# Attention and the first six expert jobs under one table of dates; routing steps on GpSimd; sums of squares in SBUF

## The chip, the cores and the metric

The kernel runs on one NeuronCore of a Trainium2 chip. The metric is the device time of one execution in microseconds (us). Engines are named as in the profile: PE is TensorE (PEld its weight loads), DVE is VectorE, ACT is ScalarE, POOL is GpSimd, SP is SyncE, which here issues most of the DMAs. Each engine works through its own instructions in program order; an instruction that waits holds up all that stand behind it.

## The reference

Attention with RMS-normalised queries and keys, whose output is the token matrix of a mixture of experts with 4 groups of 4 experts, one of the 16 chosen for each token (top group, then top expert in it).

```python
q, k: (8, 12, 448, 64); v the same              # batch, heads, sequence, head size
q_n, k_n = rmsnorm(q, g_q), rmsnorm(k, g_k)     # x / sqrt(mean(x*x) + 1e-6) * g
attn = softmax(q_n @ k_n^T / sqrt(64)) @ v
x = attn.transpose(0, 2, 1, 3).reshape(3584, 768)
g_idx = argmax(x @ w_group); e_idx = argmax(x @ w_expert[g_idx])    # both with a softmax weight
out[token] = g_w * e_w * (relu(x[token] @ w1[g, e]) @ w2[g, e])     # w1: 768 x 1024, w2: 1024 x 768
```

All inputs and the output are fp32. The kernel splits most operands into a high and a low 16-bit half and multiplies three times.

## The kernel before

**Attention** is cut into 16 units of six heads (half a batch entry). For a unit SP loads q, k and v; ACT squares q and k (`sq`), DVE adds the squares up (`red`, line 247), ACT and DVE make 1/rms of the sums (`rs1`, lines 255 and 256; `rs2`, lines 260 to 262) and DVE multiplies it in (`norm_k`, `norm_q`, line 265). The sums and 1/rms lie in 42 spare columns of one of the two PSUM banks `po` into which PE also adds up the attention's output (line 597). ACT rounds k to its high half, POOL (in places DVE) takes the low one (`kn`, line 280), and DMAs transpose. PE makes scores once for the row maximum (`pmx`, which DVE reduces, `mx`, line 480) and once for the softmax (`pss`), of which ACT takes the exponential (`p`, line 546) and POOL or DVE the low half (`pl`, line 552); PE multiplies them with v (`po`, line 597). DVE or ACT scale the result into `xm`, ACT and POOL (or DVE) split it (`xhl`, lines 660 and 664), and SP stores it to a DRAM matrix `x16`.

**Routing** follows in five groups of 128-token chunks: three of seven chunks, then three and four. For each chunk `x16` is read transposed and multiplied with the gate weights (`prl`); then one chain of 20 steps (`choices`, lines 934 to 989), of which all but two are DVE's, finds the expert, the slot in its list and the token's weight, and POOL writes them by indirect DMA to a table in DRAM (`tab`). After the third group `order.early` (DVE) picks the two fullest experts, on which work may start before the last tokens are routed. After the last group `order.final` sorts all sixteen (`order`, line 1101).

**Experts** run as 18 jobs: 0 and 1 are the early rows of the first two experts (256 and 224 rows), 2 and 3 their later rows (96 and 64), 4 to 17 one expert each. A job reads its rows' numbers (POOL, line 1287 or 1292), gathers the tokens by indirect DMA (`xg`, line 1310), transposes them by DMA into `mx` (line 1417), and PE multiplies them with w1 (line 1321) and w2 (line 1340). An expert's weights come as eight pieces of 768 KB (`stage`, line 1268) that ACT rounds to high halves (line 1274) and DVE to low halves (line 1275). Two sets of 16-bit weights take turns.

**The order of the work** is written out. Every piece of attention and routing is a task of `Flow`, which names the engine, the tasks that it follows and the buffers that it takes; the table `PLAN` gives each task a date, and a star picks its second engine. The dates set only the order in which instructions are recorded, and so their order on each engine. The expert jobs are not tasks: `Moe.plan` gives them dates of its own (`MO`, and 2.5/6 ns for each column of a matmul) beside those of the attention. The memory of the experts' first weights is opened when the last task that uses the early buffers is recorded, that of the rest after the last `po` matmul.

Of the kernel before, what the change touches and what calls it, by code (L numbers as in the profile page):

```python
# [21 lines left out]
P = 128  # L22
# [42 lines left out]
class Flow:  # L65

    def __init__(self, room):
        self.room, self.tasks = room, []  # L70
# [33 lines left out]
class Attention:  # L104
# [8 lines left out]
                psd=3, psx=2, pso=2, p=7, xm=1, hl=1, rx=2)  # L113
# [111 lines left out]
    def plan_prep(self, flow, u, B, D):  # L225
# [20 lines left out]
        def red(nm, o, a, e):  # L246
            nc.vector.tensor_reduce(rms()[:, o + a:o + e], d["sq" + nm][:, a:e], axis=AX.X, op=ALU.add)  # L247
# [3 lines left out]
        def rs1(a=0, e=N):  # L251
            if a == 0:
                d["y"] = self.wk.tile([P, 2 * N], F32, tag="y", name=f"y{u}")
            y, x = both_(d["y"], a, e), both_(rms(), a, e)
            nc.scalar.activation(y, x, AF.Ln, scale=1.0 / 1024, bias=self.eps)
            nc.scalar.activation(y, y, AF.Exp, scale=-0.5)

        def rs2(a=0, e=N):
            y, x = both_(d["y"], a, e), both_(rms(), a, e)
            nc.vector.scalar_tensor_tensor(x, x, 64e-6, y, op0=ALU.add, op1=ALU.mult)  # L260
            nc.vector.scalar_tensor_tensor(x, x, -0.5 / 1024, y, op0=ALU.mult, op1=ALU.mult)
            nc.vector.scalar_tensor_tensor(x, x, 1.5, y, op0=ALU.add, op1=ALU.mult)
# [144 lines left out]
    def plan_first(self, add, D, B, N, F, both, d):  # L407
# [12 lines left out]
        for i in range(NPR):  # L420
# [5 lines left out]
            for nm, o in (("k", N), ("q", 0)):  # L426
                x = task("sq" + nm, "ACT", pair(F["sq"], nm, a, e), [ld[nm]], takes=[B["sq" + nm]], uses=[B["n" + nm]])
# [140 lines left out]
    def plan_av(self, flow, u, B, D):  # L568
# [56 lines left out]
        for i in range(NPR):  # L625
# [10 lines left out]
            D["x"].append(flow.add(evac_on, lambda g, i=i: evac(g, i), [x], uses=[bo] + ([] if i else []),  # L636
# [43 lines left out]
    def plan(self, flow, router, order):  # L680
# [3 lines left out]
        add("ACT", lambda: nc.scalar.preload_act_table_set("natural_log_exp_and_others"))  # L684
# [9 lines left out]
        for u in range(U):  # L694
# [16 lines left out]
            Ds.append(D)  # L711
        for g, (a, e) in enumerate(router.groups):
            last = 2 * ((e * P - 1) // self.S) + 1
            if g == 3:
                self.early = add("DVE", lambda: order.early(router.bank, router.groups[2][1]), done, takes=[Buffer("psd")])
                done = [self.early, *done]
# [9 lines left out]
class Router:  # L726
# [26 lines left out]
    def init(self):  # L753
# [9 lines left out]
        self.tok = cp.tile([P, NC], I32, tag="tok", name="tok")  # L763
        nc.gpsimd.iota(self.tok, pattern=[[P, NC]], base=0, channel_multiplier=1)
# [40 lines left out]
    def plan_last(self, flow, a, e, Ds, done, room):  # L805
# [11 lines left out]
        def logits(d, wk):  # L817
# [57 lines left out]
            def sum_():  # L875
# [5 lines left out]
            t0 = [add("SP", lambda i=i, l=l: tr(i, l), [at(U - 4), at(U - 2)],  # L881
                      takes=rx if i + l == 0 else (), uses=() if i + l == 0 else rx) for i in range(2) for l in range(2)]
# [3 lines left out]
            t1 = [add("SP", lambda l=l: tr_tail(l), [at(U - 3)], takes=() if l else ry, uses=ry if l else ())  # L886
                  for l in range(2)]
# [14 lines left out]
    def plan(self, flow, a, e, stores, done, room, logits=None):  # L902

        nc = self.nc
        n = e - a
# [22 lines left out]
        def choices():  # L928
# [3 lines left out]
            v, bc = nc.vector, lambda t: t.unsqueeze(2).to_broadcast([P, S, E])  # L932
# [3 lines left out]
            v.tensor_tensor(D, L, bc(m), op=ALU.subtract)  # L936
# [13 lines left out]
            for j in range(n):  # L950
                v.tensor_tensor(oh[:, j], one[:, j, 1:, :], one[:, j, 0, :].unsqueeze(2).to_broadcast([P, G, E]), op=ALU.mult)
# [12 lines left out]
            v.tensor_tensor(q, o, oh, op=ALU.mult)  # L964
# [683 lines left out]
```

## Time and profile before

| | |
|---|---|
| time, median of three runs | 1061.61 us (1059.2 to 1064.75) |
| the profiled execution | 1068.18 us, of which the span of its instructions is 1066.4 us |
| busy in the span: PE, DVE, ACT, POOL | 922.6, 769.7, 597.4, 516.3 us |
| mean granted TensorE clock | 0.96 of full speed |
| last `po` matmul ends, first expert matmul starts | 535.1 us |
| job 6 starts on PE | 707.5 us |

A row of a group of instructions reads: line, engine, operation, out<-in by the program's names, sizes, count | busy time, mean ns of one | idle time of the engine ahead of them and what ended it. Busy times of neighbours overlap a little, since an instruction starts while the one ahead drains.

### The profile page before, as it was taken

Reading aid. Unit: us, or ns where it says so; the run is one execution under the profiler, and the core shown is the slowest. Engines: PE = TensorE matmul, PEld = TensorE weight load, DVE = VectorE, ACT = ScalarE, POOL = GpSimd, SP = SyncE. Lnnn points to the kernel's source line nnn. Section 1 sums busy time; section 2 is a strip of 40 time slices with the busy share of each in tenths; the row PEclk is TensorE's granted clock in tenths of the full one; section 3 lists DMA queues with packets and bytes.
Section 4 is the critical chain, followed back from the end, with each engine's and each line's share of the span. In section 5 each row is a group of like instructions: output and inputs, shape, how many; then the busy total and the mean of one; then the engine's idle time right before and its main releaser. Section 6 shows DMA issues by size and latency. Waiting matters only on the chain.

```text
span 1066.4 us, 27993 instructions
## 1 busy us (share of the span) xinstructions
PE 922.6 (87%) x11425; PEld 649.0 (61%) x11425; DVE 769.7 (72%) x1087; ACT 597.4 (56%) x962; POOL 516.3 (48%) x428
## 2 busy tenths in 40 slices
PE   1678899888896888977788989989999999999995
PEld 0335566545563555545575766766877777778883
DVE  5999899999899987977946256758666475766520
ACT  5757788667675775444734245544554465545520
POOL 5448888758874786554513441432612131433411
PEclk9989999989998999997889989999999999999998
DMA  6698999996997679834978399998999999999900
GB/s 168 161 196 195 185 212 198 202 196 159 200 192 156 146 170 197 131 90 77 252 178 251 107 317 295 323 241 288 296 316 245 311 259 295 308 278 299 283 29 26
DMA packets 298419, 224.74 MB, mean 211 GB/s; under 512 B 172015, under 2 KB 271333, under 8 KB 298288
## 3 DMA queue, kind: packets, MB, share of 16 engines
q1 hardware_dynamic: 288336, 199.24, 74.9%
q0 software_dynamic: 8608, 22.99, 7.0%
q8 instruction: 91, 1.49, 0.6%
q10 hardware_dynamic: 1344, 0.69, 0.3%
q14 instruction: 40, 0.33, 0.1%
HBM read 145.69 MB, written 23.41 MB: 159 GB/s over the span
## 4 chain that ended last, share of the span: by engine, by line
PE 51%; DVE 20%; DMA 12%; issue 7%; ACT 5%; SPq 3%; POOL 1%; another core or an unknown queue 1%; ACTq 0%; DVEq 0%; POOLq 0%
PE ps L1321 19%; PE ps L1340 15%; PE po L597 5%; PE pss L536 5%; DVE mx L480 4%; DMA mx<-xg 4%; PE pmx L475 3%; DVE po L247 2%; DVE w1l L1275 2%; DVE ql L308 1%; DMA xg<-x,tb 1%; DVE vl L346 1%; PE pss L531 1%; DVE qp L265 1%; DMA vn<-v 1%
## 5 line engine op out<-in xcount | busy, mean ns | idle before, releaser
L552 POOL TENSOR_TENSOR pl<-p 128x896 f16<-128x896 f32 (+1 forms) x143 | 238.1, 1681 | 132.0 <-ACT p L546 119.3
L1321 PE MATMUL ps<-mx,w1h 128*128 128x256 f16 (+6 forms) x1728 | 250.0, 261 | 15.0 <-DMA mx<-xg 10.6
L1321 PE MATMUL ps<-mx,w1l 128*128 128x256 f16 (+6 forms) x864 | 215.9, 261 | 0.0
L546 ACT ACTIVATE p<-pss 128x896 f32<-128x896 f32 (+1 forms) x177 | 153.3, 881 | 96.5 <-PE pss L536 70.4
L480 DVE TENSOR_REDUCE mx<-pmx 128x2 f32<-128x896 f32 (+1 forms) x177 | 177.7, 1033 | 18.4 <-PE pmx L475 16.3
L597 PEld LDWEIGHTS <-p 128*128 128x128 bf16 (+1 forms) x3072 | 150.7, 104 | 61.6 <-issue 40.2
L1321 PEld LDWEIGHTS <-w1h 128*128 128x128 f16 x1728 | 159.1, 100 | 34.0 <-issue 9.8
L597 PE MATMUL po<-vh,p 128*128 128x65 f16 (+1 forms) x1536 | 159.1, 200 | 13.6 <-DVE qp L265 7.4
L1340 PE MATMUL ps<-w2l,hh 128*128 128x384 f16 (+2 forms) x768 | 164.9, 303 | 3.0 <-issue 3.0
L1340 PE MATMUL ps<-w2h,hh 128*128 128x384 f16 (+2 forms) x768 | 164.4, 305 | 1.3 <-issue 1.3
L597 PE MATMUL po<-vh,pl 128*128 128x65 f16 (+1 forms) x1536 | 157.6, 197 | 8.5 <-DVE pl L552 6.5
L1340 PE MATMUL ps<-w2h,hl 128*128 128x384 f16 (+2 forms) x768 | 163.8, 303 | 0.0
L1275 DVE SCALAR_TENSOR_TENSOR w2l<-stage,w2h 128x1536 f16<-128x1536 f32 x64 | 112.3, 1754 | 64.3 <-ACT w2h L1274 63.0
L597 PE MATMUL po<-vl,p 128*128 128x64 f16 (+1 forms) x1536 | 157.8, 196 | 0.2 <-issue 0.2
L1324 ACT ACTIVATE hh<-ps 128x256 f16<-128x256 f32 (+6 forms) x144 | 49.5, 349 | 172.9 <-PE ps L1321 158.9
L1340 PEld LDWEIGHTS <-hh 128*128 128x128 f16 (+2 forms) x1536 | 101.7, 100 | 64.5 <-issue 10.6
L1275 DVE SCALAR_TENSOR_TENSOR w1l<-stage,w1h 128x1536 f16<-128x1536 f32 x64 | 112.9, 1786 | 32.4 <-ACT w1h L1274 31.7
L597 PEld LDWEIGHTS <-pl 128*128 128x128 f16 (+1 forms) x1536 | 130.1, 103 | 9.8 <-DVE pl L552 6.9
L1351 POOL DMA_INDIRECT out<-y,tb x23 | 32.2, 1401 | 201.0 <-DVE y L1346 102.5
L536 PE MATMUL pss<-qa,kt 128*128 128x448 f16 x288 | 106.5, 370 | 22.8 <-DVE mx L480 17.8
L1310 POOL DMA_INDIRECT xg<-x,tb x41 | 69.4, 1692 | 101.0 <-DMA mx<-xg 48.3
L536 PE MATMUL pss<-qb,kb 128*128 128x448 f16 x288 | 106.4, 369 | 5.8 <-DMA qb<-mxt 5.8
(195 smaller groups left out, 1525.4 us busy)
## 6 DMA issues: line engine op xcount, KB each, us to landing
stage<-w SPq DMA_DIRECT2D x128, 768.0 KB
vn<-v SPq DMA_DIRECT2D x16, 576.0 KB
x<-xhl SPq DMA_DIRECT2D x16, 576.0 KB
nk<-k SPq DMA_DIRECT2D x30, 288.0 KB
nq<-q SPq DMA_DIRECT2D x30, 288.0 KB
qa<-qh SPq DMA_DIRECT2D x30, 176.0 KB
kb<-kt SPq DMA_DIRECT2D x15, 336.0 KB
qa<-qh SPq DMA_DIRECT2D x30, 160.0 KB
```

What stands on the lines that cost most here:

```text
L475: nc.tensor.matmul(s[:, n - a, 0:448], qa[:, n * P:(n + 1) * P], kt[:, x:z], start=True, stop=True)
L480: nc.vector.tensor_reduce(d["mx"][:, a:e], d.pop(("mm", a))[:, 0:e - a, 0:448], axis=AX.X, op=ALU.max)
L536: nc.tensor.matmul(s[:, n - a, 0:448], w[:, n * P:(n + 1) * P], mv[:, x:z], start=first, stop=not first)
L546: nc.scalar.activation(p[:, 0:e - a], s, AF.Exp, scale=1.0 / 64)
L552: ENG[eng].tensor_tensor(l[:, 0:n], p[:, 0:n], h[:, 0:n], op=ALU.subtract)
L597: nc.tensor.matmul(o[op, c, 0:nn], w, mv, start=st, stop=sp, skip_group_check=True)
L1275: self.nc.vector.scalar_tensor_tensor(lo, t, 64.0, hi, op0=ALU.mult, op1=ALU.subtract)
L1310: self.nc.gpsimd.indirect_dma_start(g[0:m], None, self.x16[0:n], bass.IndirectOffsetOnAxis(ap=tb[0:m, i, 0:1], axis=0), bounds_check=n - 1 ...
L1321: nc.tensor.matmul(s[:, 0:c], wb[w][:, i, fs], x[:, l + i, o:o + c], start=i + j == 0, stop=i == DC - 1 and j == 2)
L1324: nc.scalar.activation(hh, s[:, 0:c], AF.Relu)
L1340: nc.tensor.matmul(s[q * m:q * m + m, 0:n], self.h[h][:, f, a:a + m], wb[w][:, f, o:o + n], start=f + j == 0, stop=f == self.FC - 1 and j ...
L1351: i = self.nc.gpsimd.indirect_dma_start(out, bass.IndirectOffsetOnAxis(ap=idx, axis=0), d.pop(("y", i))[:, 0:self.D // r], None, bounds_ch ...
```

## The change

What it does, part by part:

1. `Moe.plan_early` makes the first six jobs tasks of the same `Flow`, and the table `PLAN` is new for all tasks (2512 instead of 2176). The opening of the experts' memory is a task too. `Moe.plan` still dates jobs 6 to 17 as before. The weight split and the relu are cut into ACT's and DVE's part, so that each has a date of its own.
2. In `choices` six steps of each of the three groups of seven chunks go from DVE to POOL (the difference to the maximum, the product of the choices in one instruction instead of seven, two additions, one product, one cast), the test for zero and the product with the priority become one DVE instruction, and a copy is gone. `order.early` is cut into eight steps over PE, DVE and POOL.
3. The sums of squares go to an SBUF tile `ss`; the exponential in `rs1` writes 1/rms to the `po` bank, where the first guess and the result of `rs2` stay.
4. The first task on ACT loads the table set that holds both the logarithm and the exponential, and the first squares depend on it: the built program has one ACT_TABLE_LOAD instead of eight.
5. By the new table 14 of the 16 units' low halves `xhl` are POOL's (before 9), 142 of 177 `pl` (before 143), and 26 of 30 `kn` (before 27).

```diff
-        add("ACT", lambda: nc.scalar.preload_act_table_set("natural_log_exp_and_others"))
+        self.table = add("ACT", lambda: nc.scalar.preload_act_table_set("natural_log_exp_and_others"))
...
-            nc.vector.tensor_reduce(rms()[:, o + a:o + e], d["sq" + nm][:, a:e], axis=AX.X, op=ALU.add)
+            nc.vector.tensor_reduce(d["ss"][:, o + a:o + e], d["sq" + nm][:, a:e], axis=AX.X, op=ALU.add)
...
-            y, x = both_(d["y"], a, e), both_(rms(), a, e)
+            y, x, z = (both_(t, a, e) for t in (d["y"], d["ss"], rms()))
             nc.scalar.activation(y, x, AF.Ln, scale=1.0 / 1024, bias=self.eps)
-            nc.scalar.activation(y, y, AF.Exp, scale=-0.5)
+            nc.scalar.activation(z, y, AF.Exp, scale=-0.5)
...
-            v, bc = nc.vector, lambda t: t.unsqueeze(2).to_broadcast([P, S, E])
+            v, g, bc = nc.vector, nc.gpsimd if side else nc.vector, lambda t: t.unsqueeze(2).to_broadcast([P, S, E])
...
-            v.tensor_tensor(D, L, bc(m), op=ALU.subtract)
+            g.tensor_tensor(D, L, bc(m), op=ALU.subtract)
...
-            v.tensor_scalar(D, D, 0.0, None, op0=ALU.is_equal)
-            yield
-            v.tensor_tensor(c, D, self.prio.unsqueeze(1).to_broadcast([P, S, E]), op=ALU.mult)
+            v.scalar_tensor_tensor(c, D, 0.0, self.prio.unsqueeze(1).to_broadcast([P, S, E]), op0=ALU.is_equal, op1=ALU.mult)
...
-            for j in range(n):
-                v.tensor_tensor(oh[:, j], one[:, j, 1:, :], one[:, j, 0, :].unsqueeze(2).to_broadcast([P, G, E]), op=ALU.mult)
+            g.tensor_tensor(oh, one[:, :, 1:, :], one[:, :, 0, :].unsqueeze(3).to_broadcast([P, n, G, E]), op=ALU.mult)
...
-            v.tensor_scalar(s, s, 1e-9, None, op0=ALU.add)
+            g.tensor_scalar(s, s, 1e-9, None, op0=ALU.add)
-            v.tensor_tensor(self.run, self.run, r, op=ALU.add)
+            g.tensor_tensor(self.run, self.run, r, op=ALU.add)
-            v.tensor_tensor(t, one[:, :, 0, :], W[:, :, 1:], op=ALU.mult)
+            g.tensor_tensor(t, one[:, :, 0, :], W[:, :, 1:], op=ALU.mult)
-            v.tensor_copy(d["slot"], w)
+            g.tensor_copy(d["slot"], w)
-            v.tensor_copy(row[:, :, 0], self.tok[:, a:e])
...
+    EARLY = ("PE", "DVE", "DVE", "POOL", "DVE", "POOL", "DVE", "POOL")
...
+    def plan_early(self, flow, attn, router, opens):
+        m1 = add("NONE", opens[0], flow.using(early))
+        m2 = add("NONE", opens[1], [m1, *flow.using(late)])
+        m3 = add("NONE", opens[2], [m2, *flow.using(lambda b: b.kind == "pso")])
...
+                x = add("SP", lambda k=k, i=i, st=st: self.w_load(self.expert(k, nc.sync), PC[i], self.stage[st], nc.sync),
+                        [attn.early if k < 2 else attn.final, m1 if k == 0 else m2], takes=[b])
+                x = add("ACT", lambda k=k, i=i, st=st: self.w_split(wb(k), PC[i], self.stage[st], 0), [x, m1 if k == 0 else m2, *free], uses=[b])
+                x = add("DVE", lambda k=k, i=i, st=st: self.w_split(wb(k), PC[i], self.stage[st], 1), [x], uses=[b])
...
+                x = mm[j, f] = add("PE", lambda j=j, f=f, k=k, c=c, s=s: s.update(p=self.mm1(wb(k), self.xb[j % 2], f, c, self.col[j])),
+                                   [m2, sets[k][f // 2], *([*trs, *([mm[j - 1, FC - 1]] if j else [])] if f == 0 else [mm[j, f - 1]])], takes=[b])
...
-2366 0 1211 6349 10381 11581 12046 518 1563 1 2 880 945 927 1014 1083 1151 1229 1301 1400 1464* 1581 1372 1711 1811
+210 553 1020 7396 9043 13116 15028 1620 3045 0 1 424 485 486 550 731 915 1030 1136 1480 1997* 2088 1482 1615 2089 1776
```

Place one, DVE at the routing of the first group of seven chunks (`rl` are its logits, `rm` to `roh` the chain's results). Before:

```order
L934 TENSOR_REDUCE rm_3516<-rl_2476 128x35
L936 TENSOR_TENSOR rd_3517<-rl_2476,rm_3516 128x140
L346 SCALAR_TENSOR_TENSOR vl_3471<-vn_133,vh_130 128x768
L940 TENSOR_SCALAR rd_3517<-rd_3517 128x140
L942 TENSOR_TENSOR rc_3519<-rd_3517,prio 128x140
L944 TENSOR_REDUCE rcm_3520<-rc_3519 128x35
L946 TENSOR_TENSOR rd_3517<-rc_3519,rcm_3520 128x140
L308 SCALAR_TENSOR_TENSOR ql_3546<-pqt_1_3541,ghc,qh_3545 128x384
L308 SCALAR_TENSOR_TENSOR ql_3546<-pqt_0_3507,ghc,qh_3545 128x1024
L951 TENSOR_TENSOR roh_3644<-rd_3517 128x16 x7
```

DVE at the same place in the change (`rm` is 13 instructions ahead of `rc`):

```order
L356 SCALAR_TENSOR_TENSOR vl_3864<-vn_133,vh_130 128x768
L270 SCALAR_TENSOR_TENSOR ss_3719<-ss_3719,po_111 128x42
L271 SCALAR_TENSOR_TENSOR ss_3719<-ss_3719,po_111 128x42
L272 SCALAR_TENSOR_TENSOR po_111<-ss_3719,po_111 128x42
L957 SCALAR_TENSOR_TENSOR rc_3834<-rd_3832,prio 128x140
L275 TENSOR_TENSOR nk_3412<-nk_3412,po_111 128x640
L275 TENSOR_TENSOR nk_3412<-nk_3412,po_111 128x704
L959 TENSOR_REDUCE rcm_3835<-rc_3834 128x35
L612 TENSOR_SCALAR rr_2_4034<-po_112 128x7
L613 RECIPROCAL rr_2_4034<-rr_2_4034 128x7
L490 TENSOR_REDUCE mx_3717<-pmx_12_4031 128x2
L961 TENSOR_TENSOR rd_3832<-rc_3834,rcm_3835 128x140
```

POOL at that place in the change:

```order
L562 TENSOR_TENSOR pl_20_3829<-p_20_3828 128x448
L953 TENSOR_TENSOR rd_3832<-rl_2696,rm_3831 128x140
L562 TENSOR_TENSOR pl_4_3867<-p_4_3866 128x896
L562 TENSOR_TENSOR pl_0_3845<-p_0_3844 128x896
L562 TENSOR_TENSOR pl_2_3990<-p_2_3989 128x896
L562 TENSOR_TENSOR pl_6_4014<-p_6_4013 128x896
L562 TENSOR_TENSOR pl_12_4021<-p_12_4020 128x896
L965 TENSOR_TENSOR roh_4102<-rd_3832 128x112
```

The difference and the product have moved to POOL, each behind one or more `pl`; DVE's remaining steps of the chain now stand apart, with other work between.

Place two, ACT at the end of attention (`p` are the last unit's exponentials, `w1h` the first expert's weights). Before:

```order
L546 ACTIVATE p_8_9532<-pss_8_9518 128x896
L660 ACTIVATE xhl_9548<-xm_9079 128x3x384
L660 ACTIVATE xhl_9548<-xm_9079 128x192
L546 ACTIVATE p_12_9577<-pss_12_9526 128x896
L1274 ACTIVATE w1h_9198<-stage_9203 128x6x256
L546 ACTIVATE p_14_9646<-pss_14_9624 128x896
L1274 ACTIVATE w1h_9198<-stage_9204 128x6x256
L546 ACTIVATE p_16_9674<-pss_16_9649 128x896
L546 ACTIVATE p_18_9698<-pss_18_9680 128x896
L1274 ACTIVATE w1h_9198<-stage_9205 128x6x256
L546 ACTIVATE p_20_9792<-pss_20_9776 128x448
L1274 ACTIVATE w1h_9198<-stage_9206 128x6x256
```

And in the change:

```order
L556 ACTIVATE p_8_9432<-pss_8_9424 128x896
L1314 ACTIVATE w1h_9202<-stage_9209 128x6x256
L943 ACTIVATE rl_9097<-prl_9470 128x20
L556 ACTIVATE p_12_9574<-pss_12_9452 128x896
L955 ACTIVATE rx_9509<-rd_9508 128x60
L670 ACTIVATE xhl_9639<-xm_9034 128x3x384
L670 ACTIVATE xhl_9639<-xm_9034 128x192
L556 ACTIVATE p_14_9642<-pss_14_9618 128x896
L556 ACTIVATE p_16_9666<-pss_16_9645 128x896
L556 ACTIVATE p_18_9676<-pss_18_9671 128x896
L556 ACTIVATE p_20_9718<-pss_20_9715 128x448
L1314 ACTIVATE w1h_9202<-stage_9207 128x6x256
```

Three weight splits stood ahead of the last exponential; now one does, but it stands ahead of five exponentials instead of four. On DVE four low halves `w1l` stood ahead of the last `pl`, now one.

## Rows read from the trace of the kernel before

**Rows 1.** The page: busy time of PE, DVE and POOL (us, share of the span, instructions), and the shares of the chain of work that ended last.

```profile
PE 922.6 (87%) x11425; PEld 649.0 (61%) x11425; DVE 769.7 (72%) x1087; ACT 597.4 (56%) x962; POOL 516.3 (48%) x428
PE 51%; DVE 20%; DMA 12%; issue 7%; ACT 5%; SPq 3%; POOL 1%; another core or an unknown queue 1%; ACTq 0%; DVEq 0%; POOLq 0%
```

**Rows 2.** Busy time of each engine by stretches of the span: from and to, length, PE busy (instructions), PEld, DVE, ACT, POOL, granted clock, DMA share, GB/s.

```profile
0.00:72.00 72.00, 34.84 (x256) 16.83 (x256) 56.09 (x76) 44.61 (x69) 35.84 (x58) 0.93 0.73 173
72.00:200.00 128.00, 115.95 (x1807) 73.98 (x1807) 120.27 (x169) 98.99 (x183) 103.50 (x76) 1.00 0.95 196
200.00:360.00 160.00, 131.96 (x2029) 84.44 (x2027) 149.12 (x221) 108.62 (x206) 109.60 (x71) 0.94 0.87 183
360.00:535.10 175.10, 142.58 (x2340) 93.60 (x2337) 146.04 (x234) 102.60 (x192) 107.13 (x80) 0.92 0.69 152
535.10:707.50 172.40, 154.74 (x1740) 116.22 (x1736) 99.19 (x161) 78.00 (x112) 59.34 (x57) 0.95 0.84 241
707.50:1056.00 348.50, 342.56 (x3264) 263.96 (x3264) 198.64 (x230) 164.55 (x204) 99.87 (x87) 1.00 0.87 257
```

**Rows 3.** The chain of work that ended last, in order of time: start, us, what.

```profile
19.19 1.28 ACT L255
...
26.60 1.28 ACT L255
28.18 1.28 ACT L256
...
506.32 9.65 DMA stage<-w
...
535.14 5.67 PE ps L1321 x36
...
569.47 9.00 issue
578.46 3.79 DMA mx<-xg
582.39 15.64 PE ps L1321 x144
...
707.52 19.73 PE ps L1321 x144
...
1041.22 13.64 PE ps L1340 x173
```

**Rows 4.** DVE's groups of instructions, shapes apart: those of routing that the change moves or merges, the low halves that move between DVE and POOL, and the weight split.

```profile
L1275 DVE SCALAR_TENSOR_TENSOR w1l<-stage,w1h 128x1536 f16<-128x1536 f32 x64 | 112.9, 1786 | 32.4 <-ACT w1h L1274 31.7 <-issue 0.6
L346 DVE SCALAR_TENSOR_TENSOR vl<-vn,vh 128x768 f16<-128x768 f32 x32 | 37.0, 1155 | 0.0
L552 DVE TENSOR_TENSOR pl<-p 128x896 f16<-128x896 f32 x30 | 35.2, 1186 | 5.2 <-ACT p L546 5.1
...
L951 DVE TENSOR_TENSOR roh<-rd 128x16 f16<-128x16 f32 x28 | 12.4, 506 | 0.0
...
L664 DVE TENSOR_TENSOR xhl<-xm,xhl 128x1152 f16<-128x1152 f32 x7 | 9.8, 1396 | 0.0
...
L664 DVE TENSOR_TENSOR xhl<-xm,xhl 128x192 f16<-128x192 f32 x7 | 5.4, 774 | 0.0
...
L940 DVE TENSOR_SCALAR rd<-rd 128x140 f32<-128x140 f32 x3 | 3.6, 1214 | 0.0
...
L280 DVE TENSOR_TENSOR kn<-nk,kn 128x704 f16<-128x704 f32 x2 | 3.2, 1622 | 0.0
...
L982 DVE CAST slot<-rv 128x7 int32<-128x7 f32 x3 | 2.3, 777 | 0.1
L979 DVE TENSOR_TENSOR rt<-rd,rs 128x28 f32<-128x28 f32 x3 | 2.3, 760 | 0.0
...
L1085 DVE COPY ooh<-ogt 1x32 f32<-1x32 f32 x1 | 1.7, 1669 | 0.0
...
L969 DVE TENSOR_SCALAR rs<-rs 128x35 f32<-128x35 f32 x3 | 1.3, 440 | 0.0
...
L987 DVE COPY row<-tok 128x7 int32<-128x7 int32 x3 | 1.1, 373 | 0.0
```

**Rows 5.** DVE in order of time near the end of attention (start, us, instruction): the same two kinds of instruction, short and long.

```profile
516.12 1.09 DVE L552 TENSOR_TENSOR pl<-p 128x896 f16<-128x896 f32 x1
...
521.28 2.57 DVE L552 TENSOR_TENSOR pl<-p 128x896 f16<-128x896 f32 x1
...
524.08 2.93 DVE L1275 SCALAR_TENSOR_TENSOR w1l<-stage,w1h 128x1536 f16<-128x1536 f32 x1
```

**Rows 6.** POOL's groups: the low halves of p and of the output.

```profile
L552 POOL TENSOR_TENSOR pl<-p 128x896 f16<-128x896 f32 x129 | 224.8, 1758 | 119.4 <-ACT p L546 106.8 <-issue 4.3 <-DMA qa<-qh 3.6
...
L664 POOL TENSOR_TENSOR xhl<-xm,xhl 128x1152 f16<-128x1152 f32 x9 | 21.7, 2406 | 2.4 <-ACT xhl L660 2.4
...
L664 POOL TENSOR_TENSOR xhl<-xm,xhl 128x192 f16<-128x192 f32 x9 | 5.0, 556 | 0.0
```

**Rows 7.** ACT in order of time: a table load and the activation behind it.

```profile
9.40 1.28 ACT L255 ACT_TABLE_LOAD   x1 [0.18 <-DVE po L247]
10.70 0.27 ACT L255 ACTIVATE y<-po,eps 128x14 f32<-128x14 f32 x1
```

**Rows 8.** DVE in order of time: the cast with which the order of the experts is known.

```profile
581.34 0.16 DVE L1101 CAST order<-oof 1x16 int32<-1x16 f32 x1
```

More of the change, by code (lines that the diff above doesn't have):

```diff
@@ L65 @@
 class Flow:
+    TURNS = ("nv", "vh", "kt", "kb", "qa", "qb", "pso", *(f"st{i}" for i in range(7)), "gb0", "gb1")
     def __init__(self, room):
-        self.room, self.tasks = room, []
+        self.room, self.tasks, self.turn = room, [], {}
     def add(self, engines, f, deps=(), takes=(), uses=()):
@@ L77, in add, with using @@
             b.users.append(t)
+        for b in takes:
+            if b.kind in self.TURNS:
+                t.deps += [x for x in self.turn.get(b.kind, ()) if x not in t.deps]
+                self.turn[b.kind] = [t]
         self.tasks.append(t)
         return t
+    def using(self, pick):
+        return [t for t in self.tasks if any(pick(b) for b in t.uses)]
     def place(self):
@@ L714, in plan @@
             if g == 3:
-                self.early = add("DVE", lambda: order.early(router.bank, router.groups[2][1]), done, takes=[Buffer("psd")])
-                done = [self.early, *done]
+                steps, bp, x = order.early(router.bank, router.groups[2][1]), Buffer("psd"), None
+                for j, on in enumerate(order.EARLY):
+                    x = add(on, lambda: next(steps, None), [x, *([] if j else done)], takes=[] if j else [bp], uses=[bp] if j == 1 else [])
+                self.early = x
+                done = [x, *done]
             stores = lambda j, a=a: [s for b in sorted({((a + j) * P) // self.S, ((a + j + 1) * P - 1) // self.S})
@@ L1003, in plan @@
             x = add("SP", lambda j=j: tr(j), stores(j), takes=[bx])
[L1004 to L1005 removed]
+            x = add("PE", lambda j=j: mm(j), [x, self.ready, first], takes=[bp] + ([] if j else [rl]), uses=[bx])
+            first = first or x
+            cps.append(add("ACT", lambda j=j: cp(j), [x], uses=[bp, rl]))
         c = choices()
         x, bp = None, Buffer(room)
[L1008 to L1011 removed]
+        for j in range(19):
+            on = "ACT" if j == 2 else "PE" if j == 7 else "POOL" if side and j in (1, 6, 11, 12, 15, 16) else "DVE"
+            x = add(on, lambda: next(c, None), [x, *(done + cps if j == 0 else [])],
+                    takes=[bp] if j == 7 else (), uses=[bp] if j == 8 else [rl] if j < 2 else ())
+        self.puts.append([add("POOL", lambda j=j: put(j), [x]) for j in range(n)])
+        return [x, *self.puts[-1]]
 class Order:
@@ new lines, in early @@
+        ix, key = self.ix[:, 0:NE], self.key
+        sq = [1, NE, NE]
+        gt, rk, t = self.oh, self.tile("ork", [1, NE]), self.tile("pick", [1, NE, NE])
+        t2, n, s = self.tile("pick2", [1, 2, NE]), self.tile("onum", [1, NE]), self.tile("ost2", [1, 2])
+        assert r.routed == chunks
+        p = bank("pcnt")
+        nc.tensor.matmul(p[0:1, 0:NE], r.ones[:, 0:1], r.run, start=True, stop=True)
+        yield
+        v.scalar_tensor_tensor(key, p[0:1, 0:NE], 16.0, self.kb, op0=ALU.mult, op1=ALU.add)
@@ L1434, in plan @@
         for i in range(30):
-            at(T[5] + 3000.0 * i, lambda: next(rest, None))
+            at(T[6] + 3000.0 * i, lambda: next(rest, None))
     def rest(self):
@@ L1613, in body @@
         attn.plan(flow, router, order)
-        flow.place()
-        flow.emit(agenda, STEP)
-        begun = lambda pick: max(t.start for t in flow.tasks if pick(t)) / STEP
-        kinds = lambda ks: lambda t: any(b.kind in ks for b in t.uses)
-        at = agenda.at(0)
         def banks():
```

402 lines of the change are left out of this document (240 added, 162 removed), and 125 rows, old and new, of the table PLAN.

## The prediction

> **What bounds the kernel now.** I read the page first: PE is busy 87% of the span and holds half of the chain that ended last, DVE 72% and a fifth of it [rows 1]. These are means over stages, so I next cut the span where the chain changes hands: at 535.1 us, where the last attention matmul ends and the first expert matmul begins, and at 707.5 us, where job 6 starts [rows 3]. The busy times by stretch [rows 2] show three limits. From 72 to 360 us DVE is busy 120.3 + 149.1 = 269.4 of 288 us (94%), PE 247.9 (86%): attention is DVE's. From 360 to 535 us DVE falls to 146.0 of 175.1 (83%) and no engine is full: the end of attention waits. From 707.5 us on PE is busy 342.6 of 348.5 us: jobs 6 to 17 are PE's, and nothing but PE work shortens them. Between, from 535.1 to 707.5 us, PE does 154.7 us of work in 172.4 us; 9.0 + 3.8 us of its 17.7 idle us stand in one piece of the chain, from 569.5 to 582.4 us, where job 1's transposed tokens are late [rows 3].
>
> So the time is a sum of four pieces: end of attention 535.1, seam 172.4, jobs 6 to 17 348.4 (707.5 to 1055.9, the end of the last matmuls of the chain), tail 10.5 to the span's 1066.4 us. The profiled execution took 1068.2 us, 1.8 above its span and 0.6% above the median of the three runs; I make the sum against the profiled one and scale by 1061.6/1068.2 = 0.994 at the end.
>
> **DVE's work ahead of the last `po` matmul.** It sums to 56.1 + 120.3 + 149.1 + 146.0 = 471.5 us of 535.1 [rows 2]. What the change takes away, by [rows 4]:
> - Routing of the three groups of seven chunks: the test for zero, 3.6 us (merged into an instruction that is there already); 21 of the 28 `roh` products at 506 ns, 10.6; the casts 2.3, the products `rt` 2.3, the additions 1.3, the copies `row` 1.1. Together 21.2.
> - Five pairs of `xhl` go to POOL: 5 x (1.396 + 0.774) = 10.9.
> - The 1.7 us copy of `order.early`; its other steps that leave DVE are short and I leave them out.
> - Three of the four splits `w1l` ahead of the last `pl`: 3 x 1.786 = 5.4. They are late work now, and the seam has to hold them.
> - Added: one `pl`, 1.2, and one `kn`, 1.6.
>
> Net 36.4 us. The merged test-and-product keeps the price of the product that it replaces. The sums of squares I cost at nothing on DVE: the reductions read the same 1344 elements per partition, and only 21 results go elsewhere. What hides a difference there is nothing, since DVE is full, but 36 short writes cannot make 2 us. The wait for the `po` bank stays, since the exponential still writes 1/rms there.
>
> Of the table loads, three stand on the chain in the first 30 us, 1.28 us each [rows 3]: 3.8 us less. From the load to the end of waiting for it only those 1.28 us pass: the activation starts 1.30 us behind it [rows 7]. The Trainium skill says otherwise (ScalarE: Activation LUTs, What ACT_TABLE_LOAD costs): a switch costs a drain of about 1.38 us besides the load, which would make this term 8.0 us. The row shows no drain, so the row decides.
>
> Does taking away DVE work shorten attention one for one? Where DVE is 94% busy, yes. Behind 360 us not surely. From below: of the 36.4 us some 22.9 lie behind 360 us (the third of the three groups 7.1, four of the five `xhl` pairs 8.7, the copy 1.7, the splits 5.4), and if nothing of it counts, attention ends at 535.1 - 13.5 - 3.8 = 517.8. From above: all of it counts, and the stretch behind 360 us, which now idles 29.1 us on DVE, idles only the 6% of the middle, 11 us: 477. What speaks for gain there is the place where ACT stands: before, splits of `w1h` were placed between the last exponentials, and the chain runs for 9.65 us through a weight transfer [rows 3]; now one split is left ahead of them. I take one for one: 535.1 - 36.4 - 3.8 = 494.9.
>
> POOL takes the moved work: 5 x (2.406 + 0.556) = 14.8 us of `xhl` [rows 6], less one `pl` of 1.8, and some 25 small instructions that no row shows on POOL; from below nothing, from above the 556 ns of its 192-column one each, 14 us. I take 6, since most have 7 to 35 columns. POOL was busy 356 us of 535 [rows 2] and would be 375 of 495, still not full.
>
> **The seam.** The same 1120 columns of jobs, the same weights. PE's work is 154.7 us, which is the least it can take [rows 2]. At most it takes the present 172.4 plus the three splits of 1.8 us that now lie behind attention's end, 178. The new order dates the six jobs' loads, gathers and transposes beside attention's tasks, and the 12.8 us ahead of job 1 are a wait of that kind; but the weights still come only when `order.early` is done, whose eight steps now go back and forth between DVE and POOL. I take half of the idle time: 172.4 - 9 = 163.4.
>
> **Jobs 6 to 17** keep code, dates and sizes: 348.4, and the tail 10.5.
>
> Sum: 494.9 + 163.4 + 348.4 + 10.5 = 1017.2 us of span, 49.2 less than 1066.4; the profiled time 1068.2 - 49.2 = 1019.0, as a median x 0.994 = 1013 us.
>
> **The rivals.**
> - *The seam does not shrink.* Attention gains, but the six jobs wait as now, 172.4: a span of 1026.2, 1022 us. For it: the stream of weights of the other 14 experts starts when the order is known, 581.3 us [rows 8], 46.2 behind the end of attention, and runs 474.6 to the last matmul at a DMA share of 0.84 to 0.87 [rows 2]. If both stay, 494.9 + 46.2 + 474.6 + 10.5 is the same 1026.2. Against it: two of the waits are named and are not for weights.
> - *The end of attention has other limits than DVE.* Then attention ends at 517.8 and the seam stays: 1049.1, 1044 us. For it: DVE idles 17% there. Against it: so does every other engine, which speaks for an order with waits, and the order is what changes.
> - *Both go well*, 477 and 154.7: 990.6, 986 us.
> - *Slower: DVE waits for POOL.* Its place is the routing chain. Six steps in each of three groups and three of `order.early` are now POOL's, 21 hand-overs, and each time DVE, in order, stops until POOL has worked off what stands ahead, a `pl` of 1.76 us or an `xhl` pair of 2.96 [rows 6]. The gain of 49.2 us is gone when each hand-over costs DVE 2.3 us; at two `pl` each, 3.5, it is 74 us, and the time 1087. Against it: in the order DVE has 12 other instructions between `rm` and the next step that needs POOL's result, where POOL has one `pl`. A hand-over costs DVE only what POOL's backlog is longer than such a gap.
> - *Slower: the two engines lock each other out of SBUF.* The same `pl` takes DVE 1.09 us in one place and 2.57 in another, a `w1l` 2.93 where its mean is 1.79 [rows 4, 5]; the small routing steps show it worst, 1214 ns for 140 columns. With more work on POOL such stretches become more frequent. If each of the 31 `pl` and 31 `vl` of DVE took 2.57 us instead of 1.19 and 1.16, that is 87 us, and the time 1099. Against it: POOL's share of attention only goes from 67% to 76%, so a mean excess of 0.1 us a `pl` grows by an eighth. The Trainium skill has this as a rule (SBUF, State Buffer, Who interferes with whom): a DVE instruction with two SBUF inputs and a POOL instruction that reads SBUF exclude each other for a whole instruction, so that moving work to POOL makes the rest of DVE slower. The trace agrees in the long rows; it also shows that the steps which go are those that paid most.
> - *Nothing*: the bound is elsewhere, and the time stays at 1062.
>
> **Chances.** Forecast 0.55, seam unchanged 0.16, late attention unchanged too 0.12, both well 0.05, nothing 0.04, slower by hand-overs 0.06, by the lock 0.02. A difference under 0.5% is about what a measurement of this kernel cannot tell from none. Faster is 0.55 + 0.16 + 0.12 + 0.05 = 0.88, same 0.04, slower 0.08. The range goes from the good end, 986, to just past the weak gain, 1046; outside lie half of the best case, the last three and a little of the tails, some 0.17.
>
> **What would show it.** In the changed profile the last `po` matmul should end near 495 us, the `roh` product stand on POOL, DVE's busy time to that point be near 435 us; one table load; the first exponential of the last unit's end wait less for `w1h`. Job 6 should start near 658 us and 348 us later the matmuls end. It is wrong if DVE's idle time ahead of `rc`, `rq` or `rt`'s readers names POOL with tens of us, if POOL's `pl` becomes what the chain runs through, if the seam grows because the first weights land after 505 us, or if jobs 6 to 17 take other than 348 us.

## The result, and the profile after

| | before | after | forecast |
|---|---|---|---|
| median time | 1063.2 us (1059.2 to 1073.7) | 1032.4 us (1023.4 to 1037.7) | 1013 (986 to 1046) |
| the profiled execution | 1068.2 | 1037.7 | 1019 |
| end of attention (last `po` matmul) | 535.1 us | 495.7 us | 494.9 |
| seam, to the start of job 6 | 172.4 | 173.5 | 163.4 |
| jobs 6 to 17 | 348.4 | 356.3 | 348.4 |
| tail | 10.5 | 10.6 | 10.5 |

The ratio after to before, beside runs of the kernel before on the same chip, is 0.969 with a 95% interval of 0.959 to 0.979: faster by 2 to 4%. Attention ended where the forecast had it. The seam (from there to the start of job 6) did not shrink, and jobs 6 to 17 took 7.9 us more.

The page of the kernel after, the lines that answer to [rows 1]:

```profile
PE 909.3 (88%) x11425; PEld 645.7 (62%) x11425; DVE 753.2 (73%) x1015; ACT 587.9 (57%) x968; POOL 532.2 (51%) x465
...
PE 31%; DVE 24%; DMA 18%; issue 10%; POOL 6%; ACT 5%; SPq 3%; another core or an unknown queue 1%; POOLq 0%; DVEq 0%; ACTq 0%
```

PE's share of the chain fell from 51% to 31%, and DMA's rose from 12% to 18%: more of the chain now runs through transfers. (A second profile of the same kernel has 36% and 17%.) The same stretches as in [rows 2], with the borders of after:

```profile
0.00:72.00 72.00, 37.03 (x229) 18.70 (x230) 54.55 (x79) 36.72 (x56) 34.37 (x47) 0.95 0.83 188
72.00:200.00 128.00, 117.90 (x1882) 75.85 (x1881) 123.43 (x166) 101.70 (x189) 114.41 (x91) 1.00 0.90 199
200.00:360.00 160.00, 145.19 (x2342) 94.21 (x2342) 155.80 (x204) 123.91 (x246) 138.56 (x94) 0.98 0.90 196
360.00:495.60 135.60, 114.65 (x1991) 78.01 (x1984) 118.79 (x176) 82.26 (x157) 100.98 (x91) 0.94 0.74 163
495.60:669.10 173.50, 151.11 (x1742) 115.11 (x1738) 88.88 (x148) 70.79 (x113) 49.09 (x56) 0.95 0.87 241
669.10:1025.40 356.30, 343.42 (x3266) 263.86 (x3264) 211.39 (x247) 172.57 (x211) 93.81 (x87) 1.00 0.90 254
```

DVE was busy for 452.6 us up to the end of attention, not for the forecast 435; but it idled only 43.0 us there, where it had idled 63.6. From 72 to 360 us it is busy 97% of the time. In the last two rows PE is busy 151.1 and 343.4 us, where before it was 154.7 and 342.6; its idle time is 22.4 and 12.9 us, where it was 17.7 and 5.9.

Waits on the chain in the seam of after, in order of time (answers to [rows 3]): first the wait for job 2's tokens, then further tokens (`mx`, `xg`), near the end of the seam weights (`stage`).

```profile
549.88 3.67 DMA mx<-xg
553.69 3.67 PE ps L1362 x54
...
602.95 6.12 DMA mx<-xg
...
615.33 6.40 DMA xg<-x,tb
...
629.35 5.97 DMA stage<-w
...
642.08 5.06 DMA stage<-w
...
657.07 11.47 DMA stage<-w
```

DVE's groups in after (answers to [rows 4]), and POOL's new `roh`:

```profile
L562 DVE TENSOR_TENSOR pl<-p 128x896 f16<-128x896 f32 x31 | 48.1, 1565 | 7.0 <-ACT p L556 7.0
L356 DVE SCALAR_TENSOR_TENSOR vl<-vn,vh 128x768 f16<-128x768 f32 x32 | 45.3, 1420 | 0.9 <-ACT vh L350 0.9
...
L961 DVE TENSOR_TENSOR rd<-rc,rcm 128x60 f32<-128x60 f32 x1 | 5.5, 5511 | 0.0
...
L965 POOL TENSOR_TENSOR roh<-rd 128x112 f16<-128x112 f32 x3 | 1.2, 386 | 1.6 <-DVE rd L961 1.4 <-DVE rr L612 0.2
```

A `pl` on DVE takes 1.565 us instead of 1.186, a `vl` 1.420 instead of 1.155, and one `rd` of 60 columns 5.5 us.

### The profile page after: what moved, and what is told of

The parts are those of the page before. It is cut to its first block, busy times and chain, and to the rows that moved or that the text cites. A ratio compares the mean times of both kernels' runs of the same rounds, so it can differ in the third digit from the quotient of the medians.

```text
span 1036.0 us, 27917 instructions
## 1 busy us (share of the span) xinstructions
PE 909.3 (88%) x11425; PEld 645.7 (62%) x11425; DVE 753.2 (73%) x1015; ACT 587.9 (57%) x968; POOL 532.2 (51%) x465
## 4 chain that ended last, share of the span: by engine, by line
PE 31%; DVE 24%; DMA 18%; issue 10%; POOL 6%; ACT 5%; SPq 3%; another core or an unknown queue 1%; POOLq 0%; DVEq 0%; ACTq 0%
PE ps L1362 13%; PE ps L1389 11%; DVE mx L490 7%; DMA mx<-xg 5%; DMA stage<-w 3%; DVE pl L562 3%; PE po L607 3%; DMA xg<-x,tb 2%; POOL pl L562 2%; PE pss L546 2%; DVE vl L356 2%; DMA nk<-k 2%; DVE ss L259 2%; DMA nq<-q 1%; DVE w1l L1316 1%
## 5 line engine op out<-in xcount | busy, mean ns | idle before, releaser
L1316 DVE SCALAR_TENSOR_TENSOR w1l<-stage,w1h 128x1536 f16<-128x1536 f32 x64 | 110.8, 1752 | 39.9 <-ACT w1h L1314 33.3
L1314 ACT ACTIVATE w1h<-stage 128x1536 f16<-128x1536 f32 x64 | 93.8, 1480 | 74.6 <-DMA stage<-w 74.6
L1408 POOL DMA_INDIRECT out<-y,tb x23 | 35.2, 1529 | 191.4 <-ACT y L1401 93.1
L1351 POOL DMA_INDIRECT xg<-x,tb x41 | 52.1, 1271 | 138.5 <-DMA mx<-xg 82.9
L546 PE MATMUL pss<-qa,kt 128*128 128x448 f16 x288 | 103.2, 358 | 11.3 <-DVE mx L490 5.5
## 6 DMA issues: line engine op xcount, KB each, us to landing
qa<-qh SPq DMA_DIRECT2D x30, 176.0 KB
```

The source lines that it names most:

```text
L546: nc.tensor.matmul(s[:, n - a, 0:448], w[:, n * P:(n + 1) * P], mv[:, x:z], start=first, stop=not first)
L1314: self.nc.scalar.activation(hi, t, AF.Copy, scale=64.0)
L1316: self.nc.vector.scalar_tensor_tensor(lo, t, 64.0, hi, op0=ALU.mult, op1=ALU.subtract)
L1351: self.nc.gpsimd.indirect_dma_start(g[0:m], None, self.x16[0:n], bass.IndirectOffsetOnAxis(ap=tb[0:m, i, 0:1], axis=0), bounds_check=n - 1 ...
L1408: i = self.nc.gpsimd.indirect_dma_start(out, bass.IndirectOffsetOnAxis(ap=idx, axis=0), d.pop(("y", i))[:, 0:self.D // r], None, bounds_ch ...
```

## The experiments

**How far apart two profiles of the same code lie.** The changed kernel again, unaltered.

> The changed kernel unaltered, for a measure beside the next ones on the same chip and for the spread of the stages between two profiles: po ends within 3 us of 495.6, the seam within 3 of 173.4, jobs 6 to 17 within 3 of 356.2; ratio to the kernel before 0.97.

Ratio 0.971 (0.965 to 0.977), median 1030.7 us. `po` ends at 493.3, the seam takes 179.0, jobs 6 to 17 353.4; the seam thus lies outside the 3 us that I had allowed it. Seven of the profiles of this study have the same attention as the changed kernel: its two, and those of the runs below that change the work behind attention alone. Their `po` ends between 485.7 and 495.7, at 491.1 in the mean. A stage of one profile is thus known to some 5 us. The kernel before was profiled only once, in an execution at the long end of its range.

**Parts of the change alone, at the old dates.** First the routing part: six steps a group on POOL, merged as in the change.

```diff
-            v.tensor_tensor(D, L, bc(m), op=ALU.subtract)
+            g.tensor_tensor(D, L, bc(m), op=ALU.subtract)        # g: nc.gpsimd in the groups of seven
...
-            v.tensor_copy(d["slot"], w)
+            g.tensor_copy(d["slot"], w)
```

> The kernel before with only the routing part of the change: six steps a group on POOL, test and product merged, one product instead of seven; all dates stay those of before, 20 steps. Theory A (DVE's work counts one for one, wherever the dates are): 20 us off DVE, po ends near 515 instead of 535.1, time 1063 - 20 = 1043. Theory B (hand-overs cost unless dates make room for them): at the old dates each of the 18 hand-overs lets DVE wait for one pl of POOL (1.76 us) or more, 32 us or more, less 20: po ends at 545 or later, time 1070 or more.

Ratio 0.988 (0.979 to 0.997), median 1042.4 us; `po` ends at 509.6. Theory A holds: DVE's work up to there falls from 471.5 to 455.8 us, and attention is shorter by at least that (against the one long profile of before by 25.5 us; the time by 1.2%, some 13 us). The hand-overs of Theory B cost next to nothing: of all DVE's waits up to `po`'s end those for POOL are (waiting instruction, releaser, us in total, times, longest)

```profile
DVE rc L942 <- POOL rd L937: 0.3, 1, 0.3
DVE rs L973 <- POOL rs L968: 0.2, 1, 0.2
```

that is 0.5 us, at dates that were not made for it. Then the sums of squares alone, and both parts together:

```diff
-            nc.vector.tensor_reduce(rms()[:, o + a:o + e], d["sq" + nm][:, a:e], axis=AX.X, op=ALU.add)
+            nc.vector.tensor_reduce(d["ss"][:, o + a:o + e], d["sq" + nm][:, a:e], axis=AX.X, op=ALU.add)
```

> The kernel before with only the sums of squares moved to SBUF (part 3); all dates stay those of before. Undone alone in the changed kernel, this part cost about 14 us of attention, because the reductions then waited 13.8 us for the po matmuls of their bank. Theory I (it is worth something only with dates that put the reductions early): in the kernel before the reductions waited 1.1 us for that bank, so nothing is gained, po ends at 530 to 538, ratio 0.995 to 1.005. Theory J (the bank costs wherever the dates are, also through the matmuls that wait for the reductions): po ends at 525 or earlier, ratio 0.99 or less.

> The kernel before with the routing part and the sums of squares in SBUF, at the old dates: how much of the gain needs no new table. The routing part alone gave po at 509.6 us and a ratio of 0.988. By Theory I this gives the same, 507 to 513 and 0.985 to 0.99; by Theory J po ends at 500 or earlier and the ratio is 0.975 or less, which is the changed kernel's gain without its table of dates.

The sums alone: ratio 0.996 (0.992 to 0.9995), so 0.4% or some 4 us, which lies in I's range; `po` ends at 525.6, between I's 530 and J's 525, but against one long profile of before that says little. Both: `po` at 512.3, which is I's, and ratio 0.983 (0.977 to 0.989), a little below I's 0.985 and far from J's 0.975. By the means a little more than half of the gain of 3% needs no new table; with these intervals it could be a third or nearly all. What the rest is owed to (the table itself, the five `xhl`, the table loads) no run takes apart.

**Parts of the change undone, at the new dates.**

```diff
-                d["ss"], d["y"] = (self.wk.tile([P, 2 * N], F32, tag=x, name=f"{x}{u}") for x in ("ss", "y"))
+                d["ss"], d["y"] = rms(), self.wk.tile([P, 2 * N], F32, tag="y", name=f"y{u}")
```

> The changed kernel with the sums of squares and 1/rms back in the po bank, as before; all dates stay. My forecast: nothing, po ends within 2 us of 495.6, time 1032 within 5, the reductions of 1344 elements take 1.54 us either way. Rival: the reductions have to wait for the bank where the new dates do not leave room for it; then DVE idles ahead of the reductions by ten us or more and po ends behind 505.

Ratio 1.001 (0.997 to 1.006), median 1054.3 us: without this part the whole change gains nothing that can be measured. `po` ends at 510.1. The forecast of nothing was wrong, and the rival names the place. DVE's groups of reductions, in this kernel:

```profile
L259 DVE TENSOR_REDUCE po<-sqk 128x21 f32<-128x1344 f32 x15 | 23.2, 1550 | 7.4 <-PE po L607 7.0 <-ACT sqk L251 0.4
L259 DVE TENSOR_REDUCE po<-sqq 128x21 f32<-128x1344 f32 x15 | 23.2, 1550 | 7.4 <-PE po L607 6.8 <-ACT sqq L251 0.6
```

the waits between them and the `po` matmuls, in both directions:

```profile
PE po L607 <- DVE po L259: 19.9, 13, 5.1
DVE po L259 <- PE po L607: 13.8, 8, 2.9
```

and in the changed kernel:

```profile
L259 DVE TENSOR_REDUCE ss<-sqq 128x21 f32<-128x1344 f32 x15 | 23.1, 1540 | 1.5 <-ACT sqq L251 1.5
L259 DVE TENSOR_REDUCE ss<-sqk 128x21 f32<-128x1344 f32 x15 | 23.0, 1534 | 0.7 <-ACT sqk L251 0.7
```

The price of one is the same, 1.54 and 1.55 us, as forecast. But with the sums in PSUM a reduction has to wait for the `po` matmuls of its bank: 13.8 us in front of DVE, with everything behind it on that engine. And the `po` matmuls wait for the reductions, 19.9 us; in the changed kernel both waits are absent. The old dates left more room, as the same two waits in the kernel before show:

```profile
PE po L597 <- DVE po L247: 3.9, 7, 1.4
DVE po L247 <- PE po L597: 1.1, 1, 1.1
```

Next the routing part undone, and five of POOL's fourteen `xhl` back on DVE:

```diff
-        on = ... "POOL" if side and j in (1, 6, 11, 12, 15, 16) else "DVE"
+        on = ... "DVE"                                             # and g = nc.vector, seven products roh
...
-                ENG[eng].tensor_tensor(l, x, h, op=ALU.subtract)
+                ENG["DVE" if u in (7, 8, 11, 12, 14) else eng].tensor_tensor(l, x, h, op=ALU.subtract)
```

> The changed kernel with the routing steps of the three groups of seven chunks back on DVE, in the old form (test for zero apart, seven products instead of one); all dates stay. By the old prices [rows 4] that is 7.2 us of DVE work a group, 21.5 in all. Theory A (DVE's work counts one for one): the last po matmul ends at 495.6 + 21 = 517 us, and the time is 1032 + 21 = 1053 us. Theory B (the dates made the gain; DVE still idles 9% ahead of that point, and POOL, lighter by 9 us, locks DVE out less): po ends before 506, the time is under 1042. Seam and jobs 6 to 17 as in the changed kernel, 173 and 356 us.

> The changed kernel with five of the fourteen low halves xhl that POOL computes back on DVE (units 7, 8, 11, 12, 14); all dates stay. Theory A (one for one): 5 x 2.17 = 10.9 us more on DVE, po ends near 506.5, time 1043. Theory B (shared port): in the changed kernel DVE's pl takes 1.565 us instead of 1.186 and vl 1.420 instead of 1.155, since POOL is busy beside them more of the time; with 14.8 us of POOL's work gone these means fall by a third or more of that excess, and po ends within 4 us of 495.6, time 1028 to 1036.

Routing: ratio 0.988 (0.984 to 0.992), median 1041.5, `po` at 501.4, 10.3 us behind the mean of the seven. That lies between the two forecasts; the profile speaks for A's mechanism, one for one, but of a smaller sum: DVE is busy 464.4 us up to there, 11.8 more, and not 21.5. The steps were cheaper than the rows said:

```profile
L971 DVE TENSOR_TENSOR roh<-rd 128x16 f16<-128x16 f32 x21 | 2.6, 192 | 0.0
L958 DVE TENSOR_SCALAR rd<-rd 128x140 f32<-128x140 f32 x3 | 1.5, 513 | 0.0
```

The same product took 506 ns and the same test 1214 in [rows 4]. `xhl`: ratio 0.987 (0.979 to 0.995), median 1039.8, `po` at 498.2, 7.1 behind the mean. DVE gets 10.9 us more work by the old prices and is busy 6.8 us more, since `pl` falls to 1.518 and `vl` to 1.333 us, both below the range of the seven profiles (1.555 to 1.583 and 1.385 to 1.443). That is a part of Theory B: 4.1 us, some two fifths of the price, are given back, though `pl` loses only an eighth of its excess and not the third that B asked for. The time rises above B's range, so A decides the sign.

**What the seam waits for.** First the weights of the fourteen later experts left out altogether, then half of each piece:

```diff
     def w_load(self, e, piece, st, eng, part=1):                   # part 2 for the later experts
+        if part == 2:
+            return
```

```diff
+        if part == 2:
+            if nm == "w1":
+                src, dst = self.w1[bass.ds(e, 1)][:, :, f:f + P], self.staged(nm, st)[:, :, 0:P]
+            else:
+                src, dst = self.w2[bass.ds(e, 1)][:, f:f + P], self.staged(nm, st)[:, 0:1]
```

> The changed kernel, but the weights of the fourteen later experts are never loaded: their loads are left out (the splits work on what lies in the stage buffers, so the products are not the reference's). Theory W (in the seam PE waits for weights, whose stream starts when the order is known): the seam falls from 173.4 to 158 or less, near PE's 151 us of work, and jobs 6 to 17 from 356 to 345 or less. Theory T (PE waits for tokens: routing of the last chunks, two gather buffers, SP's queue): the seam stays at 165 or more; of its 31 us of PE gaps only those of jobs 4 to 6 (3.0, 6.8 and 4) go. Time by W under 1007, by T 1008 to 1022.

> The changed kernel with only half of each weight piece loaded for the fourteen later experts (128 of 256 columns or rows of each piece; the other half of the stage buffer keeps what lay there, so the products are not the reference's). Same loads at the same places, half the bytes. Theory B (the stream of weights is bound by the bytes that the DMA engines move): the seam falls as with no loads at all, to 160 or less, and jobs 6 to 17 to 346 or less. Theory Q (the stream has holes because the loads stand in SP's queue behind transposes that wait for tokens, from 531.4 to 553.2 and 554.5 to 573.5 us in the changed kernel): the holes stay, the seam stays at 166 or more, while jobs 6 to 17, where DMA is near full, fall.

None: ratio 0.948 (0.942 to 0.954), median 1005.3. Half: ratio 0.954 (0.949 to 0.960), median 1010.5. The seam and jobs 6 to 17 with no weights, then with half of them:

```profile
493.60:649.90 156.30, 146.76 (x1740) 112.02 (x1738) 92.22 (x151) 75.52 (x116) 51.96 (x55) 0.98 0.54 134
649.90:994.00 344.10, 341.00 (x3268) 262.93 (x3264) 208.38 (x244) 165.76 (x208) 99.84 (x87) 1.00 0.26 67
```

```profile
485.70:648.70 163.00, 148.24 (x1738) 113.59 (x1736) 90.96 (x150) 75.37 (x116) 52.21 (x57) 0.97 0.75 196
648.70:992.90 344.20, 341.18 (x3272) 262.94 (x3264) 208.93 (x245) 166.71 (x208) 96.75 (x87) 1.00 0.62 164
```

Against the first profile of the changed kernel weights are worth 17 us of the seam and 12 of the jobs behind it (Theory W; against its second profile 23 and 9). Half the bytes at the same places in the queue give back 10 of the 17 and all of the 12. The seam of 163.0 lies between the two theories (160 or less, 166 or more), so the bytes weigh more than the places, but the places are not shown to cost nothing.

Then the other suspects: a third gather buffer from job 2 on, and PE's order, in which job 2's first products stood ahead of job 1's last.

```diff
-M2 = (3, 0)
+M2 = (3, 1)
...
-                b = Buffer(f"gb{g % 2}")
...
+                n = g % (2 if j < 2 else 3)
+                b = Buffer(f"gb{n}")
```

```diff
 # dates in PLAN of job 2's first three w1 products (job 1's last w2 product has 51158), and of a w1h split that follows them
-49647 ... 49747 ... 49848 ... 50828
+51162 ... 51164 ... 51166 ... 51167
```

> The changed kernel with three gather buffers instead of two from job 2 on; dates stay. Theory T: POOL's gathers, which wait 55 us of the seam for a buffer to be transposed, go out earlier, the tokens of jobs 2 to 5 come earlier, and the seam shrinks by 5 us or more, to 168 or less. Theory W: the gathers go out earlier and nothing comes of it, the seam stays within 3 us of 173.4. A third outcome: the dates of the transposes on SP hold them as before, so that also the gathers' wait only moves to the transposes.

> The changed kernel, but the first three w1 products of job 2 stand behind job 1's w2 products on PE instead of ahead of them. In the changed kernel PE stands idle from 548.4 to 553.7 us with job 1's work ready behind it. Theory T: those 5.3 us are gained and job 2's tokens are there when its turn comes; seam 168. Theory W: the next wait (weights of job 4 or 5, whose loads are not earlier) takes them, seam within 2 us of 173.4.

Third buffer: ratio 0.974 (0.966 to 0.981), seam 176.0: nothing is gained, as Theory W has it. POOL's gathers wait 18.9 us for a buffer instead of 55.0, but the last two transposes of the six jobs go out 106.2 and 107.5 us behind the end of attention, where they went out at 106.0 and 107.3. That is the third outcome of the expectation: what earlier tokens would give, this run does not show. PE's order: ratio 0.967 (0.959 to 0.974), which is that of the changed kernel. The gap of 5.3 us is gone, and PE waits later instead: it idles 22.2 us in that seam, against 22.4. Its profiled execution was the longest of its four (1040.7 us, median 1027.7), so its stretches decide nothing. Last, that order with the third expert's loads moved up in SP's queue: four of them go ahead of the transposes of job 2's tokens, three right behind these:

```diff
 # dates of seven of the third expert's eight loads in PLAN (transposes of job 2: 49242, 49304)
-50189 49389 49452 53006 52985 51889 52695
+48920 48921 48922 48923 49392 49453 49742
```

> The changed kernel with two moves in its order: the first three w1 products of job 2 behind job 1's w2 products (as in the run that did this alone), and seven of the eight loads of the third expert's weights ahead of the transposes of the tokens of jobs 2 and 3 in SP's queue instead of between and behind them. Theory Q: the loads go out at about 541 us, when the order is known, instead of 553 to 580; job 4's and job 5's waits for weights shrink, seam 163 or less, time 1020 or less. Theory B: the DMA engines are no faster for it, the tokens of job 2 come later by the 10 us of bytes ahead of them, seam 173 or more.

Ratio 0.970 (0.961 to 0.978), median 1027.1: no measurable gain on the changed kernel. The loads did go out earlier, the first 46.9 us behind the end of attention instead of 57.6. The stretch from 532 to 553 us, in the changed kernel and here:

```profile
532.00:553.00 21.00, 14.76 (x132) 12.39 (x130) 15.29 (x24) 9.57 (x14) 11.00 (x15) 1.00 0.64 189
```

```profile
532.00:553.00 21.00, 18.77 (x158) 14.77 (x158) 13.47 (x24) 8.01 (x12) 12.41 (x15) 1.00 0.96 295
```

This hole in the stream is filled (DMA share 0.96 instead of 0.64; in the 20 us behind it the share is 0.81 instead of 0.91), and the seam takes 169.2 us instead of 173.5 to 179.0: some of Theory Q, but neither its 163 nor its 1020, and 4.3 us below the nearer of two seams that differ by 5.5 themselves.

## Why the prediction was right, and where it was not

- **End of attention, 494.9 forecast, 495.7 measured: the right sum of two wrong terms, which is luck.** DVE's relief was put at 36.4 us and is 18.9 by busy time (471.5 to 452.6). Against it, DVE's idle time, which I kept but for 3.8 us, fell by 20.6. The seven profiles with this attention end it at 491.1 in the mean, so even the agreement to 1 us is partly that of one profile.
- **The step that was mis-sized: what stays on DVE keeps its price.** `pl`, `vl` and one `rd` became longer by 31 x 0.379 + 32 x 0.265 + 5.3 = 25.5 us. The rival of the shared SBUF port had this mechanism and the sign, and I had set it against the sum at 2 in 100 instead of putting it into the sum. All seven `pl` and all twelve `vl` above 1.5 us in attention overlap a `TENSOR_TENSOR` on POOL, and each ends at a fixed distance behind the end of one: `pl` 0.94 to 0.96 us, `vl` 0.81 to 0.82, as if it had run only once POOL's was through. (Overlap alone says little: 27 of the 44 shorter ones overlap one too.) The Trainium skill's rule (SBUF — State Buffer, Who interferes with whom), by which a DVE instruction with two SBUF inputs and a POOL instruction that reads SBUF shut each other out for a whole instruction, is borne out by this. Its consequence for a plan, that work moved to POOL can slow what stays on DVE, belongs in the sum. What the rival had too high was the price, 87 us, since 44 of the 63 still run at 1.1. With 25.5 us off, the relief would be 10.9; the other 8.0 are spread over steps that I left out or priced too low, the largest the `roh` products, of which 13.5 us left and not 10.6.
- **The step that was wrong: the sums of squares "at nothing".** I counted their work, which did not change, and not the waits that they take away, 13.8 us of DVE's and 19.9 of PE's at the new dates. There this part is worth the whole measured gain, at the old ones 0.4%. "The wait for the `po` bank stays" was true at the old dates alone: ACT waits 16.9 us for `po` matmuls before making 1/rms in the kernel before, 14.1 with only the sums in SBUF, and not at all in the changed kernel.

```profile
ACT y L255 <- PE po L597: 16.9, 9, 3.2
```

```profile
ACT po L256 <- PE po L597: 14.1, 9, 3.1
```

- **Prices of moved steps.** Rows of before are prices at the place where a step stood. The steps of routing cost 21.2 us by [rows 4]; put back into the changed kernel they cost 11.8.
- **Hand-overs: rightly held unlikely.** DVE waits for a result of POOL nowhere in the attention of the changed kernel, and for 0.5 us at the old dates.
- **Seam, 163.4 forecast, 173.5 measured: the step "half of the idle time" failed.** The rival "the seam does not shrink" came true in its size, but its reason misread the trace: the stream of the later weights does not start when the order is known. The order is known at 581.3 us before and 540.4 now, 46.2 and 44.7 behind the end of attention, as that rival had it. But the third expert's first load goes out behind transposes in SP's queue, at 607.5 before and 553.2 now (the two lines below). That is 72.4 us behind the end of attention before and 57.5 now: the stream starts 15 us earlier, and the seam is no shorter for it. When the first load goes out another 10.7 us earlier, the seam is 169.2, no further from 173.5 than two profiles of one kernel are apart. Fewer bytes do shorten it, by 10 us with half of them. What spoke against the rival, two waits for tokens, was a gap that PE spends elsewhere when it is closed. PE's 154.7 us were not the least either: 151.1 now, 146.8 without weights. Behind the end of attention the chip moves 41.8 + 90.5 = 132 MB in 530 us (173.5 x 241 and 356.3 x 254 GB/s), and before 41.5 + 89.6 = 131 MB in 521 us [rows 2]: the same bytes at the same 250 GB/s. Why the mean rate stays there, with the start moved and a hole filled, is open.

```profile
607.55 3.23 SPq L1268 DMA_DIRECT2D stage<-w  x4
```

```profile
553.20 1.71 SPq L1307 DMA_DIRECT2D stage<-w  x3
```

- **Jobs 6 to 17, 348.4 forecast, 356.3 measured: the assumption that unchanged code keeps its time failed.** The four profiles with the old table have them at 345.5 to 350.3 us, those with the new one and all weights at 352.7 and more. They begin with their weights less far ahead: in the first 51 us PE is busy 46.4, where before it was 50.7 in as long a stretch (the two lines below). With half of the weights they take 344.2. Nothing in the rivals had this; the term "474.6 us from order to end" could have, as it measured 484.9.

```profile
707.50:758.50 51.00, 50.74 (x441) 36.83 (x442) 36.35 (x51) 24.20 (x30) 18.96 (x12) 1.00 0.87 285
```

```profile
669.00:720.00 51.00, 46.42 (x385) 32.29 (x380) 40.38 (x52) 28.79 (x30) 13.38 (x12) 1.00 0.94 294
```

- **Table loads** were not tried apart; 3.8 us is less than two profiles of one kernel differ by.

## What to carry to other kernels

An edit that changes no instruction's price can still be worth a lot, if it takes away a dependency that keeps an instruction in a place: ask of every operand which bank or buffer it shares, and with whom, and what a new order would do with the freedom. Parts of a change are not a sum: undone one at a time, by ratio (0.988, 0.987 and 1.001 against 0.97), the three cost 2, 2 and 3% here (by their medians, taken on another chip, 1, 1 and 2%), of a gain of 3%. And when the end of a first stage comes earlier, find the stream that feeds the next stage, the row where it really starts and its rate, before crediting the gain to the end.

## What the runs showed of the hardware

A DVE instruction can be held up by POOL for far longer than one instruction of POOL. In the changed kernel one `pl` of 128x896, which takes 1.1 us alone, took 9.07. DVE and POOL in that stretch, in order of time:

```profile
331.41 9.07 DVE L562 TENSOR_TENSOR pl<-p 128x896 f16<-128x896 f32 x1
```

```profile
330.11 6.60 POOL L562 TENSOR_TENSOR pl<-p 128x896 f16<-128x896 f32 x4
336.66 2.86 POOL L290 TENSOR_TENSOR kn<-nk,kn 128x704 f16<-128x704 f32 x2
```

The `pl` begins 0.3 us before the second of six POOL instructions that follow each other without a gap, and ends 1.0 us behind the last of them. It is there in all kernels with the new table (9.1 to 9.5 us) and in none with the old one. The `rd` of 5.5 us lies likewise beside two `xhl` and two `pl`. In elsewhere equal attention the two profiles in which that `rd` takes 1.7 to 1.8 us have `po` end at 485.7 and 486.8, and the five in which it takes 5.4 to 5.5 at 490.4 to 495.7. Why DVE gets its turn after one instruction in most places and only after a whole run of them in these two stays open, and a table that keeps two-input work of DVE out of POOL's runs was not tried.
